# Attention and MLP in one kernel: the first unit's keys split ahead of their square sums, the first pair's left rows loaded alone, two weight loads and the LayerNorm scaling moved on GpSimd's queue, and the last tile stored in three groups

## The chip, the cores and the metric

The kernel runs on one core of a Trainium2 chip. The metric is the device time of one execution in microseconds. A profile is one execution taken by the hardware profiler; its times count from the first instruction (the span). In what follows PE is the matrix engine, DVE the vector engine, ACT the scalar engine, POOL is GpSimd, and SP the engine that mostly issues DMAs. PSUM is the memory that PE writes.

## The reference

```
q_n, k_n = rmsnorm(q, g_q), rmsnorm(k, g_k)        # over head_dim = 64
attn = softmax(q_n @ k_n.T / sqrt(64))
x = (attn @ v), heads side by side                 # batch 8, seq 448, 12 heads -> 768 columns
xn = (x - mean) / sqrt(var + 1e-6) * g_ln
out = x + relu(xn @ w_ch1) @ w_ch2                 # 768 -> 3072 -> 768
```

All inputs and the output are float32. The kernel works in float16 with float32 sums: keys are split into a high and a low half, so that the product with the queries loses little.

## The kernel before, in words

**Work.** Heads are handled in pairs, 6 pairs for each of 8 batches, 48 in all (p = 0 to 47). The tokens of a head are 384 "main" rows (three tiles of 128) and 64 "left" rows. The left rows of the two heads of a pair share one tile of 128. The inputs of one or two pairs form a unit u, which is loaded and prepared together: units 0 and 1 have one pair, all others two.

**Preparing a unit** is a set of one-letter steps (`pieces`, line 185): `b` begins; `a` and `c` square the keys and the queries on ACT (line 210); `d` and `e` sum the squares on DVE (L213); `gk`, `gq` or `g` take the inverse roots on ACT (L216, L218); `i` multiplies the keys by g_q times g_k, on DVE for units 0 to 2 and on POOL after that (L223; in unit 0 it first makes that product, L222); `j` rounds the keys to their high half, on POOL for units 1 to 4 and on ACT otherwise (L229, L231); `k` subtracts it to make the low half on DVE (L234); `l` scales the queries on DVE (L67); `m` duplicates them on DVE or POOL (L273); `z` casts the values on POOL (L279, L285).

**Attention of a pair.** `K` and `Q` transpose keys and queries on PE (L307 to L324) and copy them out of PSUM (L312 on DVE, L327 on ACT or L329 on DVE). `S p.i` multiplies one tile of keys by the queries (L346, or L349 and L350 for the left rows) and takes the exponential on ACT (L352, out to the tile E). Two PSUM buffers hold the scores, so a score waits until ACT has read the one two before. `V p.i` multiplies E by the values (L375, L377), and after the seventh the result is divided by its sums on DVE (L390 to L397).

**MLP of a batch.** `T` takes statistics (L528), `A` and `N` make the normalized rows on DVE (L543, L548, which read `gln`), `X` transposes them, and `R` takes the root. The first three blocks of the first product are written out as `U` (L642), the others are L599 with the ReLU at L601. The second product is L612: for each token tile and each half of 384 columns, 24 matmuls; then DVE adds the residual (L616) and the tile is stored (`store`). In the last batch the last tile (the left rows of two batches) comes last, in two halves of 384 columns, each stored by two DMAs on SP's queue (L657).

**What sets the order.** The first attention, up to the MLP of batch 0, is written out by hand in the list `ORDER`: it is walked once, and each engine executes its own share in that order. From then on the attention of batch b + 1 is woven into the MLP of batch b in steps. `load_first` (line 137) issues the loads of batch 0: ACT's queue takes the first pair's keys, SP's queue all else. Here the keys' and queries' left rows of all six pairs come in one call, which is two DMAs (one for each head of a pair, L135). In `ORDER`, `G` loads `gln`, `G2` scales it on POOL (L424), `L4` to `L7` load units 4 to 7 on SP, and `W0`, `W1`, `W2` load the thirds of w_ch1 from POOL's queue (L502); the halves of w_ch2 follow later (L507). At the end `flag` counts values that are out of bounds; its result decides whether a slow general version runs (it doesn't with these inputs). Two of its operations (L707, L709) are placed by the scheduler in DVE's stream right behind the first `i0`.

Each DMA from SP's or ACT's queue signals on one of eight semaphores, taken in turn. A DMA that takes a semaphore again waits on its queue until the earlier DMA on it has landed. In the kernel before, the first eight (the first pair's loads, all left rows, and g_q and g_k) wait for nothing.

Of the kernel before, what the change touches and what calls it, by code (L numbers as in the profile page):

```python
# [8 lines left out]
FP32 = mybir.dt.float32  # L9
FP16 = mybir.dt.float16  # L10
INT32 = mybir.dt.int32
ALU = mybir.AluOpType
AFT = mybir.ActivationFunctionType
AX = mybir.AxisListType
ENG = mybir.EngineType
PSUM = bass.MemoryType.PSUM
ts = bass.ts

B, H, S, D = 8, 12, 448, 64
DM, FF = 768, 3072  # L20
NDC, NFF = DM // 128, FF // 128
NPAIR = H // 2
# [11 lines left out]


ORDER = """
b0 c0 e0 a0 d0 b1 i0 gq0 a1 G L4 L5 j0 z0 k0 gk0 l0 i1 m0 d1 c1 K0 Q0 e1 b2 j1 g1 a2 S0.0 S0.1
S0.2 l1 m1 k1 c2 S0.3 d2 K1 e2 S0.4 V0.0 i2 S0.5 Q1 g2 j2 l2 V0.1 S0.6 S1.0 S1.1 S1.2 m2 b3
V0.2 a3 z2 V0.3 k2 c3 S1.3 S1.4 K2 V0.4 V0.5 Q2 V0.6 V1.0 S1.5 i3 W0 d3 S1.6 V1.1 e3 V1.2 S2.0
T0 V1.3 S2.1 K3 S2.2 Q3 S2.3 V1.4 S2.4 z3 V1.5 V1.6 S2.5 S2.6 V2.0 S3.0 g3 S3.1 V2.1 S3.2 j3  # L40
W1 k3 W2 G2 V2.2 l3 b4 S3.3 m3 S3.4 Q4 V2.3 V2.4 a4 K4 S3.5 V2.5 V2.6 S3.6 Q5 V3.0 S4.0 S4.1
K5 d4 c4 V3.1 V3.2 i4 V3.3 S4.2 V3.4 V3.5 S4.3 V3.6 V4.0 S4.4 S4.5 V4.1 S4.6 e4 j4 T1 V4.2 k4
g4 S5.0 S5.1 V4.3 V4.4 V4.5 l4 S5.2 S5.3 S5.4 K6 V4.6 S5.5 V5.0 V5.1 m4 z4 L6 b5 V5.2 S5.6 a5
i5 V5.3 V5.4 V5.5 Q6 V5.6 T3 S6.0 S6.1 S6.2 S6.3 T5 S6.4 V6.0 A V6.1 N0 V6.2 N1 V6.3 S6.5 V6.4
S6.6 X0 X1 U0 V6.5 c5 N2 X2 d5 U1 U2 R e5 V6.6 g5 j5 k5 l5 m5 z5 L7
""".split()
DMA_UNIT = 8
PE_SET = (DMA_UNIT + 1) % 2
# [4 lines left out]
K_MAX = 6.0e4  # L53
# [22 lines left out]
class _Fast:  # L76
# [60 lines left out]
    def load_first(self):  # L137
        nc = self.nc
        flat = self.hT.rearrange("p f n -> p (f n)").bitcast(FP32)
        t = [flat[:, 2688 * n:2688 * n + 2688].rearrange("p (w g d) -> p w g d", w=NPAIR, d=D)  # L140
             for n in range(2)]
        flat = self.sh.w2.rearrange("p f n -> p (f n)").bitcast(FP32)
        t.append(flat[:, 128:128 + 2688].rearrange("p (w g d) -> p w g d", w=NPAIR, d=D))
        main = lambda eng, n, p: self.load_main(eng, n, t[n][:, p, 0:6], 0, 2 * p, 2)
        left = lambda eng, n: self.load_left(eng, n, t[n][:, :, 6], 0, 0, H)
        for n, eng in ((0, nc.sync), (1, nc.scalar)):
            main(eng, n, 0)
            left(eng, n)
        for n in range(2):
            nc.sync.dma_start(self.sh.gg[:, n], self.gs[n].unsqueeze(0).broadcast_to([128, D]))  # L150
        for n, p in ((1, 1), (0, 1), (1, 2), (1, 3), (0, 2), (0, 3), (2, 0), (2, 1)):
            main(nc.sync, n, p)
        left(nc.sync, 2)
        for n, p in ((1, 4), (1, 5), (0, 4), (0, 5)):
            main(nc.sync, n, p)
        for p in range(2, NPAIR):
            main(nc.sync, 2, p)
        self.v_first = t[2]
        for u, (b, hs, m) in enumerate(UNITS):
            if b == 0:  # L160
                self.loads[u] = [x[:, hs // 2:hs // 2 + m].rearrange("p w g d -> p (w g) d")
                                 for x in t]
# [22 lines left out]
    def pieces(self, u):  # L185

        nc, sh = self.nc, self.sh
        m = UNITS[u][2]
        mh, g = 2 * m, 7 * m
# [16 lines left out]
        def square(n):  # L206

            o = c["khl" if n == 1 else "qn"].rearrange("p g e d -> p (g e d)").bitcast(FP32)
            c["sq", n] = o.rearrange("p (g d) -> p g d", d=D)
            nc.scalar.activation(c["sq", n], c["t"][n], AFT.Square)  # L210

# [7 lines left out]

        def kg():  # L220
            if u == 0:
                nc.vector.tensor_tensor(out=sh.gprod, in0=sh.gg[:, 0], in1=sh.gg[:, 1], op=ALU.mult)  # L222
            (nc.vector if u in DVE_KG else nc.gpsimd).tensor_tensor(  # L223
                out=c["t"][1], in0=c["t"][1],
                in1=sh.gprod.unsqueeze(1).broadcast_to([128, g, D]), op=ALU.mult)
# [63 lines left out]
        def vall():  # L289
# [7 lines left out]
                    e=lambda: total(0), gq=lambda: root(0), gk=lambda: root(1), g=root, i=kg,  # L297
# [109 lines left out]
    def first_attention(self):  # L407
        nc, gln = self.nc, self.sh.gln
        self.batch(0)
        self.load_first()  # L410
        nc.scalar.add_instruction(mybir.InstLoadActFuncSet(
            name=nc.get_next_instruction_name(), act_func_set_id=LN_EXP_SET))
        nc.scalar.activation(self.sh.warm, self.sh.ones, AFT.Ln)
        ln = {}
        for x in ORDER:
            key, n = x[0], x[1:]
            if x == "S6.0":
                self.batch(1)
            if key == "L":
                self.load_unit(int(n))  # L420
            elif x == "G":
                nc.sync.dma_start(gln, self.g_ln.unsqueeze(0).broadcast_to([128, DM]))
            elif x == "G2":
                nc.gpsimd.tensor_scalar(out=gln, in0=gln, scalar1=XS, scalar2=None, op0=ALU.mult)  # L424
            elif key == "W":
                c = int(n)
                self.load_w1(1024 * c, 1024 * c + 1024) if c < 3 else self.load_w2(c - 3)
            elif key in "SV":
                (self.scores if key == "S" else self.values)(*map(int, n.split(".")))
            elif key in "KQT":  # L430
                dict(K=self.trans_k, Q=self.trans_q, T=self.stats)[key](int(n))
            elif key in "ANXR":
                ln = ln or self.ln_ops(0)
                ln[x]()
            elif key == "U":
                self.up_first(int(n))
            elif key == "H":
                ps = self.ps_m.tile([128, 512], FP32, tag="mlp", name="psW")
                for _ in range(int(n)):
                    nc.tensor.matmul(ps[:, 0:384], self.sh.id16,  # L440
                                     self.v16.rearrange("p s h j d -> p (s h j d)")[:, 0:384],
                                     start=True, stop=True)
            else:
                self.prep_ops(int(x[-1]))[x[:-1]]()
# [143 lines left out]
    def mlp_chunks(self, b):  # L588

        nc, sh = self.nc, self.sh  # L590
        tiles = self.tok_tiles(b)
        n = len(tiles)
        N = 128 * n
        xnT, hT = self.xnT, self.hT

        def up(f):
# [4 lines left out]
            nc.scalar.activation(out=hT[:, f, 0:N], in_=ps[:, 0:N], func=AFT.Relu)  # L601

        cur = {}
        order = [(t, g) for g in range(2) for t in range(n)] if b == 0 else [
            (t, g) for t in range(n) for g in range(2)]

        def down(t, g, s):
            if s == 0:
                cur["ps"] = self.ps_m.tile([128, 512], FP32, tag="mlp", name="psC")
            ps = cur["ps"]  # L610
            for f in range(6 * s, 6 * s + 6):
                nc.tensor.matmul(ps[:, 0:384], hT[:, f, ts(t, 128)], sh.w2[:, f, ts(g, 384)],  # L612
                                 start=(f == 0), stop=(f == NFF - 1))
            if s == 3:
                x = tiles[t]
                nc.vector.scalar_tensor_tensor(  # L616
                    out=x[:, ts(g, 384)], in0=ps[:, 0:384], scalar=self.rs[:, b, t:t + 1],
                    in1=x[:, ts(g, 384)], op0=ALU.mult, op1=ALU.add)
                if t == n - 1:
                    self.store(b, t, g)  # L620
                elif g == 1:
                    self.late.append((b, t, 2))
            elif s == 1:
                for a in self.late:
                    self.store(*a)
                self.late = []
# [2 lines left out]
            yield 6 * N / 2.4, (lambda f=f: up(f))  # L629
        for t, g in order:  # L630
            for s in range(4):
                yield 6 * 160, (lambda t=t, g=g, s=s: down(t, g, s))

    def up_first(self, t):

# [9 lines left out]
            if t == 2:  # L645
                nc.scalar.activation(out=self.hT[:, f, 0:384], in_=ps[:, 0:384], func=AFT.Relu)

    def store(self, b, t, g):

        nc, out = self.nc, self.out  # L650
        cols = slice(0, DM) if g == 2 else slice(384 * g, 384 * g + 384)
        x = (self.xs[b][:, t] if t < 3 else self.xls[b // 2])[:, cols]
        if t < 3:
            nc.sync.dma_start(out[b, 0:384].rearrange("(p j) d -> p j d", j=3)[:, t, cols], x)
        else:
            for e in range(2):
                nc.sync.dma_start(out[b - 1 + e, 384:448, cols], x[64 * e:64 * e + 64])  # L657


    def upto(self, target):  # L660
# [40 lines left out]
    def flag(self):  # L701
# [2 lines left out]
        nc, sh = self.nc, self.sh  # L704
        n = B * NPAIR * 8
        rec = self.rec.rearrange("p n t e -> p (n t e)")
        nc.vector.tensor_reduce(out=sh.gmax, in_=sh.gprod, axis=AX.X, op=ALU.max,  # L707
                                apply_absolute_value=True)
        nc.vector.tensor_scalar(out=sh.gmax, in0=sh.gmax, scalar1=1.0 / K_MAX, scalar2=None,  # L709
                                op0=ALU.mult)  # L710
        good = self.p_m.tile([128, n], FP32, tag="xn", name="good", bufs=4)
        cnt = self.fix.tile([128, 3], FP32, name="cnt", tag="cnt")
        nc.vector.tensor_scalar(out=good, in0=rec, scalar1=REC_LO, scalar2=None, op0=ALU.is_ge)
# [202 lines left out]
```

## Time and profile before

| | us |
|---|---|
| median of 7 runs (lowest, highest) | 619.29 (618.34, 620.86) |
| time of the profiled execution | 623.42 |
| its span | 621.4 |
| PE busy in the span | 584.2 (94%) |
| ACT busy, DVE busy, POOL busy | 362.0, 290.2, 184.4 |
| mean granted PE clock | 0.988 |

A timeline line gives the start, the busy time, the engine, the source line, the operation, output<-inputs, shapes, how many instructions are merged, and in brackets how long the engine sat idle before and what ended that. SPq, POOLq and ACTq lines are DMAs being issued. In a line of windows the first numbers are the window and its length, then each engine's busy time, then the granted PE clock. A line of the waits names who waited for whom, the total, the number of times and the longest.

### The profile page before, as it was taken

The numbers are of one execution on the slowest core, as the hardware profiler recorded it, in microseconds if no ns is written. First come the engines' busy times: TensorE is split into PE (matmuls) and PEld (weight loads), VectorE is DVE, ScalarE is ACT, GpSimd is POOL, SyncE is SP. The second block draws the span as 40 slices with busy tenths as digits, with TensorE's granted clock in tenths as the row PEclk, the third lists the DMA queues.
The fourth block names the chain that finished last, engine by engine and source line by source line (L and its number), as shares of the span: only waits on it lengthen the run. The fifth ranks groups of instructions, "written<-read, shape, count | busy, mean of one in ns | idle before, by whom it ended". The sixth has DMA issues, their size and how long they took to land.

```text
span 621.4 us, 11453 instructions
## 1 busy us (share of the span) xinstructions
PE 584.2 (94%) x4476; PEld 345.9 (56%) x4476; DVE 290.2 (47%) x614; ACT 362.0 (58%) x697; POOL 184.4 (30%) x239
## 2 busy tenths in 40 slices
PE   1777999989999999999999999999999999999995
PEld 0455666645556666655556666655556666654563
DVE  4778867632454544652454544652454422450011
ACT  3978887517875189717775289627765277214200
POOL 0653432204535066605435066605422000000000
PEclk9979999989999999999999999999999999999998
DMA  7999499754387366757379495748434340030011
GB/s 187 265 193 224 109 221 220 157 144 129 87 81 180 110 149 147 150 130 143 77 79 174 115 149 149 147 129 147 101 53 109 90 61 2 26 102 0 2 52 55
DMA packets 131437, 75.29 MB, mean 121 GB/s; under 512 B 97456, under 2 KB 121680, under 8 KB 131376
## 3 DMA queue, kind: packets, MB, share of 16 engines
q1 hardware_dynamic: 114384, 45.38, 36.3%
q0 software_dynamic: 15920, 28.71, 20.9%
q8 instruction: 37, 0.61, 0.4%
q10 hardware_dynamic: 1072, 0.39, 0.2%
q14 instruction: 24, 0.20, 0.1%
HBM read 52.36 MB, written 11.01 MB: 102 GB/s over the span
## 4 chain that ended last, share of the span: by engine, by line
PE 87%; DVE 5%; ACT 3%; issue 1%; DMA 0%; ACTq 0%; DVEq 0%
PE psC L612 34%; PE psH L599 34%; PE psS L346 8%; PE oA L375 5%; PE oB L377 2%; PE psS L349 1%; PE psS L350 1%; ACT E L352 1%; DVE khl L234 1%; PE tr L310 1%; DVE ssq L213 1%; ACT qn L210 1%; DVE x L392 1%; DVE qn L67 1%; ACT khl L210 0%
## 5 line engine op out<-in xcount | busy, mean ns | idle before, releaser
L599 PE MATMUL psH<-xnT,w 128*128 128x512 f16 (+1 forms) x1134 | 243.5, 354 | 2.2 <-DMA xnT<-xn 2.2
L352 ACT ACTIVATE E<-psS,rr_all 128x448 f16<-128x448 f32 x336 | 207.2, 635 | 52.2 <-PE psS L346 45.5
L612 PE MATMUL psC<-w,hT 128*128 128x384 f16 x1344 | 234.6, 326 | 0.0
L601 ACT ACTIVATE hT<-psH 128x512 f16<-128x512 f32 (+1 forms) x189 | 104.0, 551 | 129.6 <-PE psH L599 126.9
L612 PEld LDWEIGHTS <-hT 128*128 128x128 f16 x1344 | 126.1, 98 | 75.7
L599 PEld LDWEIGHTS <-w 128*128 128x128 f16 x1134 | 102.9, 98 | 84.1 <-issue 4.8
L346 PE MATMUL psS<-qU,kU 128*128 128x448 f16 x288 | 101.6, 360 | 9.2 <-ACT E L352 7.5
L375 PEld LDWEIGHTS <-E 128*128 128x128 f16 x1008 | 71.2, 99 | 49.7 <-issue 3.9
L223 POOL TENSOR_TENSOR qkv<-qkv,gprod 128x896 f32<-128x896 f32 x21 | 43.8, 2087 | 98.4 <-ACT khl L210 54.6
L375 PE MATMUL oA<-v,E 128*128 128x65 f16 x864 | 67.3, 195 | 0.9 <-DVE x L392 0.8
L616 DVE SCALAR_TENSOR_TENSOR x<-psC,rs_all,x 128x384 f32<-128x384 f32 x48 | 29.0, 616 | 70.8 <-PE psC L612 70.3
L390 DVE RECIPROCAL rec_all<-oA 128x6 f32<-128x6 f32 x48 | 9.3, 195 | 98.4 <-PE oA L375 98.2
L377 PE MATMUL oB<-v,E 128*128 128x65 f16 x288 | 52.0, 194 | 0.1
L127 POOL DMA_DIRECT2D qkv<-in_k_dram x14 | 11.2, 801 | 134.5 <-ACT E L352 72.0
L213 DVE TENSOR_REDUCE ssq<-khl 128x14 f32<-128x896 f32 (+1 forms) x25 | 26.2, 1046 | 44.1 <-ACT khl L210 44.0
L346 PEld LDWEIGHTS <-kU 128*128 128x128 f16 x288 | 28.4, 99 | 26.5 <-issue 8.1
L213 DVE TENSOR_REDUCE ssq<-qn 128x14 f32<-128x896 f32 (+1 forms) x25 | 26.2, 1047 | 27.3 <-ACT qn L210 27.1
L67 DVE SCALAR_TENSOR_TENSOR qn<-qkv,rq 128x256 f16<-128x256 f32 (+1 forms) x72 | 26.8, 429 | 22.0 <-ACT rq L218 22.0
L377 PEld LDWEIGHTS <-E 128*128 128x128 f16 x336 | 32.7, 97 | 0.5 <-DVE xl L397 0.2
L392 DVE TENSOR_TENSOR x<-oA,rec_all 128x384 f32<-128x384 f32 x48 | 26.8, 558 | 1.5
L234 DVE TENSOR_TENSOR khl<-qkv,khl 128x896 f16<-128x896 f32 x21 | 22.8, 1084 | 8.0 <-ACT khl L231 5.7
L528 DVE BATCH_NORM_STATS2 stat<-x 128x6 f32<-128x256 f32 x72 | 26.1, 416 | 0.7
(99 smaller groups left out, 447.9 us busy)
## 6 DMA issues: line engine op xcount, KB each, us to landing
out_dram<-x SPq DMA_DIRECT2D x20, 384.0 KB, 2.5
qkv<-in_k_dram POOLq DMA_DIRECT2D x14, 384.0 KB, 3.9
qkv<-in_q_dram POOLq DMA_DIRECT2D x14, 384.0 KB, 5.1
qkv<-in_v_dram POOLq DMA_DIRECT2D x14, 384.0 KB, 6.4
w<-in_moe_w_ch_dram POOLq DMA_DIRECT2D x3, 1536.0 KB, 17.2
w<-in_moe_w_ch_dram POOLq DMA_DIRECT2D x2, 2304.0 KB, 29.2
qkv<-in_k_dram SPq DMA_DIRECT2D x7, 384.0 KB, 6.0
qkv<-in_q_dram SPq DMA_DIRECT2D x7, 384.0 KB, 5.5
```

The lines of the kernel that those rows point to most:

```text
L67: nc.vector.scalar_tensor_tensor(out=out, in0=x, scalar=8.0, in1=r.unsqueeze(2).broadcast_to([x.shape[0], g, D]), op0=ALU.mult, op1=ALU.mult)
L213: nc.vector.tensor_reduce(out=c["ssq"][:, n], in_=c["sq", n], axis=AX.X, op=ALU.add)
L223: (nc.vector if u in DVE_KG else nc.gpsimd).tensor_tensor(out=c["t"][1], in0=c["t"][1], in1=sh.gprod.unsqueeze(1).broadcast_to([128, g, D] ...
L234: nc.vector.tensor_tensor(out=c["khl"][:, :, 1], in0=c["t"][1], in1=c["khl"][:, :, 0], op=ALU.subtract)
L346: nc.tensor.matmul(ps[:, 0:S], c["main"][:, ts(i, 128)], q[:, ts(h, S)], start=True, stop=True)
L352: nc.scalar.activation(out=c["E"][:, i], in_=ps[:, 0:S], func=AFT.Exp, scale=self.rr[:, g:g + 1], bias=EXP_BIAS)
L375: nc.tensor.matmul(oA[:, t, cs], E[:, i, ts(t, 128)], rhs, start=(i == 0 and t == 0), stop=(i == 6 and t == 2))
L377: nc.tensor.matmul(oB[:, cs], E[:, i, 320:448], rhs, start=(i == 0), stop=(i == 6))
L392: nc.vector.tensor_tensor(out=x[:, :, 128 * hp:128 * hp + 128].rearrange("p t (e d) -> p t e d", e=2), in0=oA[:, :, :, 0:D], in1=rec[:, 0: ...
L599: nc.tensor.matmul(ps[:, 0:N], sh.w1[:, dc, ts(f, 128)], xnT[:, dc, 0:N], start=(dc == 0), stop=(dc == NDC - 1))
L601: nc.scalar.activation(out=hT[:, f, 0:N], in_=ps[:, 0:N], func=AFT.Relu)
L612: nc.tensor.matmul(ps[:, 0:384], hT[:, f, ts(t, 128)], sh.w2[:, f, ts(g, 384)], start=(f == 0), stop=(f == NFF - 1))
```

## The change

The diff, cut to its core. `ORDER` first:

```diff
-b0 c0 e0 a0 d0 b1 i0 gq0 a1 G L4 L5 j0 z0 k0 gk0 l0 i1 m0 d1 c1 K0 Q0 e1 b2 j1 g1 a2 S0.0 S0.1
-S0.2 l1 m1 k1 c2 S0.3 d2 K1 e2 S0.4 V0.0 i2 S0.5 Q1 g2 j2 l2 V0.1 S0.6 S1.0 S1.1 S1.2 m2 b3
-V0.2 a3 z2 V0.3 k2 c3 S1.3 S1.4 K2 V0.4 V0.5 Q2 V0.6 V1.0 S1.5 i3 W0 d3 S1.6 V1.1 e3 V1.2 S2.0
-T0 V1.3 S2.1 K3 S2.2 Q3 S2.3 V1.4 S2.4 z3 V1.5 V1.6 S2.5 S2.6 V2.0 S3.0 g3 S3.1 V2.1 S3.2 j3
-W1 k3 W2 G2 V2.2 l3 b4 S3.3 m3 S3.4 Q4 V2.3 V2.4 a4 K4 S3.5 V2.5 V2.6 S3.6 Q5 V3.0 S4.0 S4.1
-K5 d4 c4 V3.1 V3.2 i4 V3.3 S4.2 V3.4 V3.5 S4.3 V3.6 V4.0 S4.4 S4.5 V4.1 S4.6 e4 j4 T1 V4.2 k4
-g4 S5.0 S5.1 V4.3 V4.4 V4.5 l4 S5.2 S5.3 S5.4 K6 V4.6 S5.5 V5.0 V5.1 m4 z4 L6 b5 V5.2 S5.6 a5
+b0 a0 c0 G L4 L5 i0 j0 e0 k0 gq0 l0 b1 m0 a1 c1 K0 Q0 d0 gk0 S0.0 S0.1 i1 e1 d1 g1 z0 j1 l1 m1
+k1 b2 a2 S0.2 c2 S0.3 d2 K1 e2 S0.4 V0.0 i2 S0.5 Q1 g2 j2 l2 V0.1 S0.6 S1.0 S1.1 S1.2 m2 b3
+V0.2 a3 z2 V0.3 k2 c3 S1.3 S1.4 K2 V0.4 V0.5 Q2 V0.6 V1.0 S1.5 i3 W0 d3 j3 S1.6 V1.1 e3 V1.2
+S2.0 T0 V1.3 S2.1 K3 S2.2 Q3 S2.3 V1.4 S2.4 z3 V1.5 V1.6 S2.5 g3 S2.6 V2.0 S3.0 S3.1 V2.1 S3.2
+k3 V2.2 l3 b4 S3.3 m3 S3.4 V2.3 V2.4 a4 K4 Q4 S3.5 V2.5 V2.6 S3.6 Q5 V3.0 S4.0 S4.1 K5 d4 c4
+V3.1 V3.2 i4 W1 V3.3 S4.2 V3.4 V3.5 S4.3 V3.6 V4.0 S4.4 S4.5 V4.1 S4.6 e4 j4 W2 T1 V4.2 k4 g4
+S5.0 S5.1 V4.3 V4.4 V4.5 l4 S5.2 S5.3 S5.4 K6 V4.6 S5.5 V5.0 V5.1 m4 z4 G2 L6 b5 V5.2 S5.6 a5
 i5 V5.3 V5.4 V5.5 Q6 V5.6 T3 S6.0 S6.1 S6.2 S6.3 T5 S6.4 V6.0 A V6.1 N0 V6.2 N1 V6.3 S6.5 V6.4
-S6.6 X0 X1 U0 V6.5 c5 N2 X2 d5 U1 U2 R e5 V6.6 g5 j5 k5 l5 m5 z5 L7
+S6.6 X0 X1 U0 V6.5 c5 N2 X2 d5 U1 U2 R e5 V6.6 g5 j5 k5 l5 m5 z5 L7 M
```

`M` is the two operations at L707 and L709, taken out of `flag`. The loads:

```diff
-        left = lambda eng, n: self.load_left(eng, n, t[n][:, :, 6], 0, 0, H)
+        left = lambda eng, n, p=0, m=NPAIR: self.load_left(eng, n, t[n][:, p:p + m, 6], 0, 2 * p, 2 * m)
         for n, eng in ((0, nc.sync), (1, nc.scalar)):
             main(eng, n, 0)
-            left(eng, n)
+            left(eng, n, 0, 1)
+        left(nc.scalar, 1, 1, NPAIR - 1)
         for n in range(2):
             nc.sync.dma_start(self.sh.gg[:, n], self.gs[n].unsqueeze(0).broadcast_to([128, D]))
-        for n, p in ((1, 1), (0, 1), (1, 2), (1, 3), (0, 2), (0, 3), (2, 0), (2, 1)):
+        main(nc.sync, 1, 1)
+        left(nc.sync, 0, 1, NPAIR - 1)
+        for n, p in ((0, 1), (1, 2), (1, 3), (0, 2), (0, 3), (2, 0), (2, 1)):
             main(nc.sync, n, p)
```

The keys' squares of unit 0 go to a place of their own, because the high half of the keys is now written before their sum is taken:

```diff
             o = c["khl" if n == 1 else "qn"].rearrange("p g e d -> p (g e d)").bitcast(FP32)
+            if u == 0 and n == 1:
+                o = self.hT.rearrange("p f n -> p (f n)").bitcast(FP32)[:, 5376:5376 + g * D]
```

The last tile of the last batch (second halves split in two, one of each two stores on ACT's queue):

```diff
+            (t, g) for t in range(n) for g in (
+                ((0, 384), (384, 192), (576, 192)) if (b, t) == (B - 1, n - 1)
+                else ((0, 384), (384, 384)))]
...
-                    self.store(b, t, g)
+                    self.store(b, t, cols, nc.scalar if b == B - 1 else nc.sync)
...
-                nc.sync.dma_start(out[b - 1 + e, 384:448, cols], x[64 * e:64 * e + 64])
+                (eng if e else nc.sync).dma_start(out[b - 1 + e, 384:448, cols],
+                                                  x[64 * e:64 * e + 64])
```

Read engine by engine, DVE's stream differs in the first unit (the sums d0, e0 and d1 and the product i1 stand later), in `M`, in the order of the copies of Q4 and K4 and in one more L616 at the end. PE's stream differs in that K4 now stands ahead of Q4 and behind V2.3 and V2.4, and in the last tile. On POOL, j3 stands ahead of z3, W1 behind i4, W2 behind j4, and G2 behind z4. On ACT, a0 and c0 change places, the keys' root of unit 0 stands behind the copy of Q0, the root of unit 3 two exponentials earlier, and ACT issues two loads more at the start and three stores at the end; the first-pair loads on SP are shorter, with two more behind k's second pair. By the turn of the semaphores, g_k's load now waits for the landing of the first pair's main key rows, and ACT's last load for that of the main query rows.

More of the change, by code (lines that the diff above doesn't have):

```diff
@@ L221, in kg @@
             if u == 0:
-                nc.vector.tensor_tensor(out=sh.gprod, in0=sh.gg[:, 0], in1=sh.gg[:, 1], op=ALU.mult)
+                nc.vector.tensor_tensor(out=sh.gprod, in0=sh.gg[:, 0], in1=sh.gg[:, 1],
+                                        op=ALU.mult)
             (nc.vector if u in DVE_KG else nc.gpsimd).tensor_tensor(
@@ L434, in first_attention @@
                 ln[x]()
+            elif key == "M":
+                gmax = self.sh.gmax
+                nc.vector.tensor_reduce(out=gmax, in_=self.sh.gprod, axis=AX.X, op=ALU.max,
+                                        apply_absolute_value=True)
+                nc.vector.tensor_scalar(out=gmax, in0=gmax, scalar1=1.0 / K_MAX, scalar2=None,
+                                        op0=ALU.mult)
             elif key == "U":
@@ L603, in mlp_chunks @@
         cur = {}
-        order = [(t, g) for g in range(2) for t in range(n)] if b == 0 else [
-            (t, g) for t in range(n) for g in range(2)]
+        order = [(t, g) for g in ((0, 384), (384, 384)) for t in range(n)] if b == 0 else [
+            (t, g) for t in range(n) for g in (
+                ((0, 384), (384, 192), (576, 192)) if (b, t) == (B - 1, n - 1)
+                else ((0, 384), (384, 384)))]
         def down(t, g, s):
+            cols = slice(g[0], g[0] + g[1])
             if s == 0:
@@ L611, in down @@
             for f in range(6 * s, 6 * s + 6):
-                nc.tensor.matmul(ps[:, 0:384], hT[:, f, ts(t, 128)], sh.w2[:, f, ts(g, 384)],
+                nc.tensor.matmul(ps[:, 0:g[1]], hT[:, f, ts(t, 128)], sh.w2[:, f, cols],
                                  start=(f == 0), stop=(f == NFF - 1))
@@ L616, in down @@
                 nc.vector.scalar_tensor_tensor(
-                    out=x[:, ts(g, 384)], in0=ps[:, 0:384], scalar=self.rs[:, b, t:t + 1],
-                    in1=x[:, ts(g, 384)], op0=ALU.mult, op1=ALU.add)
+                    out=x[:, cols], in0=ps[:, 0:g[1]], scalar=self.rs[:, b, t:t + 1],
+                    in1=x[:, cols], op0=ALU.mult, op1=ALU.add)
                 if t == n - 1:
-                    self.store(b, t, g)
-                elif g == 1:
-                    self.late.append((b, t, 2))
+                    self.store(b, t, cols, nc.scalar if b == B - 1 else nc.sync)
+                elif cols.stop == DM:
+                    self.late.append((b, t, slice(0, DM)))
             elif s == 1:
@@ L631, in mlp_chunks @@
             for s in range(4):
-                yield 6 * 160, (lambda t=t, g=g, s=s: down(t, g, s))
+                yield 6 * g[1] / 2.4, (lambda t=t, g=g, s=s: down(t, g, s))
     def up_first(self, t):
@@ L646, in up_first, with store @@
                 nc.scalar.activation(out=self.hT[:, f, 0:384], in_=ps[:, 0:384], func=AFT.Relu)
-    def store(self, b, t, g):
+    def store(self, b, t, cols, eng=None):
         nc, out = self.nc, self.out
-        cols = slice(0, DM) if g == 2 else slice(384 * g, 384 * g + 384)
         x = (self.xs[b][:, t] if t < 3 else self.xls[b // 2])[:, cols]
@@ L706, in flag @@
         rec = self.rec.rearrange("p n t e -> p (n t e)")
[L707 to L710, printed above, removed]
         good = self.p_m.tile([128, n], FP32, tag="xn", name="good", bufs=4)
```

## The prediction

> **What bounds the kernel now.** I read the slices first.
>
> ```profile
> PE   1777999989999999999999999999999999999995
> ...
> ACT  3978887517875189717775289627765277214200
> ...
> PEclk9979999989999999999999999999999999999998
> ```
>
> From the fourth slice (62 us) PE is busy without a break, and nothing of the change touches its work there but the last tile. So the change is worth what it moves in the first 62 us and in the tail. Of the waits on PE between 62 and 611 us only one is over 1 us (2.2, at 131.9), and all issues there hang on earlier work; what the first 62 us gain is therefore passed on, if the weights still come in time.
>
> The windows of the first stage show where those 62 us are loose:
>
> ```profile
> 33.00:36.50 3.50, 1.85 (x13) 0.66 (x11) 3.43 (x4) 3.47 (x9) 3.48 (x4) 1.00 0.97 151
> 36.50:40.50 4.00, 2.52 (x28) 2.30 (x28) 2.38 (x4) 0.97 (x2) 3.35 (x2) 0.53 1.06 195
> 40.50:44.00 3.50, 3.50 (x35) 2.61 (x33) 2.14 (x6) 2.02 (x4) 0.00 (x0) 0.56 1.13 211
> 44.00:50.00 6.00, 4.24 (x59) 2.62 (x56) 5.78 (x11) 5.75 (x13) 0.93 (x1) 1.00 1.12 212
> ```
>
> Columns are PE, its weight loads, DVE, ACT, POOL, the clock. Before 36.5 and after 44 DVE and ACT are full. Between them ACT works 2.99 of 7.5 us and the clock is at half. The timelines of the engines tell why:
>
> ```profile
> 33.92 1.75 DVE L234 TENSOR_TENSOR khl<-hT,khl 128x896 f16<-128x896 f32 x1
> 35.60 1.70 DVE L67 SCALAR_TENSOR_TENSOR qn<-hT,rq 128x896 f16<-128x896 f32 x1
> 37.34 0.59 DVE L273 COPY qn<-qn 128x896 f16<-128x896 f16 x1
> ...
> 33.70 1.65 POOL L502 DMA_DIRECT2D w<-in_moe_w_ch_dram  x2
> 35.38 2.29 POOL L424 TENSOR_SCALAR gln<-gln 128x768 f32<-128x768 f32 x1
> ...
> 37.98 0.29 PE L321 MATMUL psQ<-id,qn 128*128 128x128 f16 x1 [2.02 <-DVE qn L273]
> ...
> 40.51 0.63 ACT L352 ACTIVATE E<-psS,rr_all 128x448 f16<-128x448 f32 x1 [3.04 <-PE psS L346]
> ```
>
> The three DVE steps of unit 3 (k3, l3, m3) take 1.75, 1.70 and 0.59; the same shapes stand elsewhere, with POOL idle, at 1.08, 1.08 and 0.39. Beside them POOL issues W1 and W2 and scales `gln`. PE waits 2.02 us for m3, because Q4 stands ahead of V2.3, V2.4 and K4, then runs at half clock (448 columns at 0.58 instead of 0.35), and ACT waits 3.04.
>
> **The middle (W1, W2, G2, Q4, j3, g3).** DVE is continuous from 29.37 to 33.89 (chain of waits), so k3 still starts at 33.92 in this profile's clock. Starts are 1.01 apart at full speed (62.16, 63.16 for the sums of this size; 66.18, 67.19 for k and l): k3 33.92, l3 34.93, m3 35.94 to 36.34, against 37.93 now: 1.6 earlier. PE does V2.3 and V2.4 (0.22) behind S3.4 (35.61), K4 at 36.4, Q4 at 36.95 (0.55 each at the full clock, as at 29.74 and 30.32), S3.5 at 37.5 instead of 39.89. ACT ends a4 at 37.47 in both, so the first exponential comes at 37.75 instead of 40.51. From there both bounds go on: DVE has the two copies (0.66, 0.62), the division after V2 (1.32), the copies of Q5 and K5, d4 (1.09), the division after V3, e4, and reaches the end of e4 at about 45.0 instead of 48.19, with ACT's five exponentials behind c4 done at 44.9. I take **-3.2**. Ends: -1.6 if only m3's own gain comes through (half clock as now), -4.8 if DVE also loses all its idle time between 37.93 and 48.19 (10.26 less 7.1 busy, plus 1.6).
>
> The half clock is part of this. It was granted from 36.75, after 3.4 us in which PE worked 1.64; the next-emptiest stretches of that length before 60 us, 2.2 to 2.4 busy, kept the full clock. With V2.3, V2.4 and K4 in the gap the stretch 33.3 to 36.75 has about 2.2, so I expect the full clock; where the 3.4 us fall is chance, and I give the half clock 20%. The Trainium skill ("TensorE: Matmul & The Clock Gate", "Why this matters for your kernels") says that gaps up to about 3 us between bursts do no harm; here a gap of 2.02 us among thin work went with a drop, so the row and the page differ. By the page the clock would have nothing to do with the gap and the middle would be worth its lower end.
>
> **What the moved work costs where it goes.** j3 (0.94) now runs at 31.4, after d3's end at 30.46, and z3 behind it to 33.85: free before k3. W1 and W2 are one issue each (0.83 to 1.02). W1 goes behind i4 (37.5 to 39.7), W2 behind j4, which waits for d4. Queued behind them are j4 and m4; DVE at those times does PSUM copies, divisions and sums, which the trace shows at equal length with POOL busy or idle (L392 0.56 always, L213 1.07 to 1.09). W0, issued at 30.32, lands at 43.45, W1 at 50.93, W2 at 58.62, one after the other at a full DMA share; W2 issued at 44 is still ahead of its turn. The eighth and sixteenth block of L599 need them after 70 and 80 us. Cost 0; if the cover were gone, the first would be late by what W1 lands after 67.
>
> G2 (2.29) behind z4 delays i5 and z5. Measured from l4's end at 51.16, m4, z4 and G2 take 0.94 + 1.5 + 2.29 and end at 55.9, 1.4 ahead of N0 (57.30), which reads `gln`. But i5 (2.08) now runs 55.9 to 58.0 and z5 (1.49) until 59.5, beside N0, N1 and N2 (0.95 each). DVE operations with two inputs in SBUF beside a POOL cast took 1.09 (L234, 72.61) or 1.46 (L67, 73.88) instead of 1.08; beside i's product no row shows one. N1 leads to X1 and U0, N2 has 1 us to spare. I take **+0.3**, nearest to the row at 73.88; ends 0 and +1.3 (all three at 1.6 times). The Trainium skill ("SBUF — State Buffer", "two separate sides") calls the shared port an exclusive lock that is held for a whole instruction. Here l3, started 0.22 after G2, ended 0.37 before it, so it was slowed, not shut out. By the page N1 would wait out casts already begun, and the term would be near +1.3.
>
> `M` (0.21 + 0.15) leaves the first unit, where L709 ended at 11.71 while k0 waited for ACT until 12.05, and goes behind m5 at 69.1; DVE has 0.52 idle in the next 4 us (before 71.66 and 72.61). Cost 0, at most +0.36 if d6 and e6 pass it on.
>
> **The start.** Four lines carry it:
>
> ```profile
> 10.51 0.23 DVE L222 TENSOR_TENSOR gprod<-w 128x64 f32<-128x64 f32 x1 [2.17 <-DMA w<-in_g_k_dram]
> ...
> 15.87 0.83 POOL L279 CAST v<-w 128x768 f16<-128x768 f32 x1 [14.55 <-DMA w<-in_v_dram]
> ...
> 17.75 0.56 POOL L229 CAST khl<-hT 128x448 f16<-128x448 f32 x1
> ...
> 18.34 0.95 DVE L234 TENSOR_TENSOR khl<-hT,khl 128x448 f16<-128x448 f32 x1 [1.17 <-POOL khl L229]
> ```
>
> Everything waits for g_k (issued 3.61, landed 6.8 later). Its issue now waits for the key rows, 0.75 + 3.9 = 4.65; on the other hand 256 packets of left rows, not 1536, are ahead of it (the DMA share falls only at 5.5), and the two g loads then took 2.4 to 2.8 from first to last. I estimate g_q landing at 7.2 and g_k at 9.5, 0.9 earlier; ends 1.1 later (the issue's delay) and 1.1 earlier. ACT's table load moves behind the second load's wait (4.3 + 0.64), 1.28 + 0.2, so its first square still starts near 6.5. From gprod to the first score now 5.45 us; without i1 (0.62) between l0 and m0 it is 4.9.
>
> But unit 1 takes the gain back: its k1 waits for j1, which POOL does behind z0, and z0 waits for the values. Their loads are issued behind one more wait for g_k (q2's turn) and two more left loads of 0.6 each, so they land about when they do now: I estimate 0.3 earlier. K1 (19.34) and all after it gain **-0.3**; ends -1.1 and +2.4 (the issue 1.1 later and 1.3 of two more places in the queue).
>
> **The tail.** Two lines of the timeline and one of the waits:
>
> ```profile
> 611.45 5.01 SPq L657 DMA_DIRECT2D out_dram<-xl  x4
> 614.70 0.62 DVE L616 SCALAR_TENSOR_TENSOR xl<-psC,rs_all,xl 128x384 f32<-128x384 f32 x1 [3.28 <-PE psC L612]
> ```
>
> ```profile
> SPq L884 <- SPq L884: 2.6, 1, 2.6
> ```
>
> After the last add SP issues two stores (615.35 to 616.46), branches, waits 2.6 and leads the end. Now the add has 192 columns: L67 took 0.42 for 256 and 0.285 for 128, 1.05 ns a column, so 0.2 less. SP issues one store, 0.59 less. 48 matmuls of 192 columns in place of 24 of 384 cost PE nothing if the pitch halves; transposes of 128 columns with a weight load each come every 0.057, so 0.08 is free; I allow +0.06. But ACT now reads the flag and branches behind its own store: 615.7 + 0.54, then up to 3.46 as PE's branch took: 619.7, about when SP is done. I take **-0.6**; ends -0.9 and 0.
>
> **Sum.** -0.3 - 3.2 + 0.3 - 0.6 = -3.8. The profiled execution took 623.42 (span 621.4 and 2.0 around it), 4.1 over the median 619.29; it would take 619.6, and the median **615.5**.
>
> **Rivals.**
> 1. *The clock still drops*, at another place in the thin stretch. Then the middle is worth 1.6 and the sum is -2.2: **617.1**. For it: PE stays thin from 33.5 to 36.4. Against: K4 comes 1.6 before Q4 did.
> 2. *The start pays as well and a second drop goes.* The half clock at 135.7 (3.4 us, so 1.7 lost) follows PE's wait of 2.2 at 131.9, and may miss it by chance: -1.1 - 3.2 - 0.6 - 1.7 = -6.6, **612.7**.
> 3. *The load queue holds up the values: slower.* The waits for g_q and g_k stand in front of k3 and q2, and so of all that is behind them on SP. If the values' left rows, now 16.65, land later by L, K1 is later by L, unit 2's loads too. Against the 3.5 gained elsewhere it decides from L = 3.5, landing at 20.2; it is slower by over 0.2% from 21.4. At 22.5, say: +5.8 - 3.5 = +2.3, **621.6**. Against: my bound is 2.4.
> 4. *The first 62 us don't pass it on*: ACT's chain at 67 to 74 or the load of w_ch2 (landed 96.42, needed at 99.3) takes it back; only the tail remains: **618.7**.
>
> **Chances.** Forecast 60%, from 614 to 617 by itself; rival 1 16%, rival 2 8%, rival 3 8%, rival 4 8%. 0.2% is 1.2 us, about what the runs can tell from no change. Rivals 3 and 4 split: slower 8%, same 9% (618.05 to 620.5), faster 83%. The range leaves out rival 3 and the far ends of 2 and 4: 612.9 to 618.8.
>
> **What would show it.** Right: L234 and L67 of unit 3 at 1.08, K4 ahead of Q4 with no wait over 0.5, the clock at 1.0 from 36 to 44, the end of e4 about 3.5 us earlier, K1 near 19.0, one store on SP behind the last add. Wrong: a clock of half there, values landing after 17.5, N0 to N2 at 1.5 each, PE waiting for w in L599 or L612.

## The result and the profile after

The changed kernel takes 616.85 us (median of 19 runs, 614.73 to 618.87), the kernel before 619.21 in the same comparison. The ratio is 0.9961, 95% interval 0.995 to 0.9971, or 2.4 us less (1.8 to 3.1). The forecast was 615.5, with 614 to 617 as its own range.

The profiled execution of the changed kernel took 619.82, with a span of 618.1 (before: 623.42 and 621.4). The slices of the page show the same picture as before from the fourth slice on, where PE is full:

```profile
PE   1687999999999999999999999999999999999995
...
ACT  3896887527765399627765399527765377214200
...
PEclk9898999999999999999999999999999999999998
```

Four windows of the first stage follow (columns PE, its weight loads, DVE, ACT, POOL, the clock, then the DMA share and GB/s). The first two are at the times of the two half-clock windows of before:

```profile
36.50:40.50 4.00, 3.72 (x53) 2.70 (x51) 3.48 (x8) 3.94 (x8) 1.34 (x1) 1.00 1.13 214
40.50:44.00 3.50, 2.74 (x45) 1.95 (x43) 3.34 (x8) 3.50 (x7) 2.49 (x4) 1.00 0.52 70
...
53.40:57.70 4.30, 2.26 (x37) 1.37 (x35) 4.30 (x9) 2.79 (x5) 4.24 (x4) 1.00 1.11 223
57.70:61.10 3.40, 3.40 (x38) 3.40 (x36) 0.88 (x2) 1.65 (x2) 0.71 (x1) 0.50 1.11 276
```

The hole at 36 to 44 is gone: ACT works 7.44 of 7.5 us where it worked 2.99, at the full clock. But there is a new half clock at 57.7, after a stretch in which PE works half of the time. Two groups of timeline lines, DVE's and PE's, show the middle as it is now:

```profile
35.26 1.09 DVE L240 TENSOR_TENSOR khl<-hT,khl 128x896 f16<-128x896 f32 x1
36.27 1.08 DVE L67 SCALAR_TENSOR_TENSOR qn<-hT,rq 128x896 f16<-128x896 f32 x1
37.39 0.39 DVE L279 COPY qn<-qn 128x896 f16<-128x896 f16 x1
...
37.59 0.22 PE L313 MATMUL tr<-id,khl 128*128 128x128 f16 x1
...
37.98 0.22 PE L327 MATMUL psQ<-id,qn 128*128 128x128 f16 x1
```

k3, l3 and m3 take 1.09, 1.08 and 0.39, and PE goes from K4 to Q4 without a wait. Yet k3 starts at 35.26, 1.34 later than before. The lines of the first unit and of POOL tell where the first 0.7 of it comes from; the other 0.6 is a half clock between K1 and k3:

```profile
9.47 0.23 DVE L227 TENSOR_TENSOR gprod<-w 128x64 f32<-128x64 f32 x1 [6.60 <-DMA w<-in_g_k_dram]
...
16.57 0.83 POOL L285 CAST v<-w 128x768 f16<-128x768 f32 x1 [15.25 <-DMA w<-in_v_dram]
...
18.45 0.56 POOL L235 CAST khl<-hT 128x448 f16<-128x448 f32 x1
...
20.05 0.29 PE L313 MATMUL tr<-id,khl 128*128 128x128 f16 x1 [3.15 <-DVE khl L240]
```

The g weights come 1.04 earlier, but the values 0.70 later (their first load is issued at 10.64 instead of 8.79), and everything behind them (z0, j1, k1, K1) moves with the values: K1 starts at 20.05 instead of 19.34. Adding up the pair of profiled executions by what starts when:

| stretch | before | after | difference |
|---|---|---|---|
| up to K1 | 19.34 | 20.05 | +0.7 |
| K1 to k3 | 14.58 | 15.21 | +0.6 (half clock at 26.98 to 30.4) |
| k3 to the end of e4 | 14.27 | 10.01 | -4.3 |
| end of e4 to N0 | 9.11 | 9.12 | 0 |
| N0 to the end of N2 | 2.81 | 3.86 | +1.05 |
| end of N2 to the first L599 (now L611) | 3.55 | 4.76 | +1.2 (half clock at 57.7 to 61.1) |
| from there to the sixth of DVE's adds (L616, now L631), 132 | 68.75 | 68.56 | -0.2 |
| to the seventh, 180 | 50.37 | 47.88 | -2.5 (no half clock at 136: 1.7; PE's wait there 0.8 shorter) |
| to the end | 438.65 | 438.60 | -0.05 |

From the seventh add to the first half of the last tile every add keeps its distance in all profiles of this study to 0.02 us; all differences lie ahead of 180 us and in the tail.

The -2.5 in the last row but one is not the change's. From the first L599 to the seventh add the kernel before takes 119.12 us and the changed one 116.44; but r5 below, which has the old order everywhere up to there, takes 116.66, and e1, with the changed one, 117.36. PE's wait at 131 us is for a DMA transpose and scatters alike with the old order and the new: 2.21 before, 1.45 in r5, 1.41 in the changed kernel, 2.15 in e1. Of the 3.4 us between the two profiled spans some 0.9 are left for the change, the 1.8 that its two half clocks take included.

### The profile page after: what moved, and what is told of

It reads as the page before. It is cut to its first block, busy times and chain, and to the rows that moved or that the text cites. A ratio compares the mean times of both kernels' runs of the same rounds, so it can differ in the third digit from the quotient of the medians.

```text
span 618.1 us, 11521 instructions
## 1 busy us (share of the span) xinstructions
PE 582.2 (94%) x4500; PEld 347.9 (56%) x4500; DVE 290.0 (47%) x615; ACT 361.8 (59%) x697; POOL 186.2 (30%) x239
## 4 chain that ended last, share of the span: by engine, by line
PE 86%; ACT 5%; DVE 4%; DMA 1%; issue 1%; SPq 0%; ACTq 0%; DVEq 0%
PE psC L627 34%; PE psH L611 34%; PE psS L352 7%; PE oA L381 5%; ACT E L358 2%; PE oB L383 2%; PE psS L355 1%; PE psS L356 1%; DMA qkv<-in_k_dram 1%; PE psU L657 1%; ACT qn L215 1%; PE tr L316 1%; DVE khl L240 0%; DVE xn L560 0%; DVE x L398 0%
## 5 line engine op out<-in xcount | busy, mean ns | idle before, releaser
L611 PE MATMUL psH<-xnT,w 128*128 128x512 f16 (+1 forms) x1134 | 242.1, 353 | 1.4 <-DVE x L631 1.4
L627 PE MATMUL psC<-w,hT 128*128 128x384 f16 (+1 forms) x1368 | 234.6, 323 | 0.0
L627 PEld LDWEIGHTS <-hT 128*128 128x128 f16 x1368 | 127.7, 98 | 74.2
L611 PEld LDWEIGHTS <-w 128*128 128x128 f16 x1134 | 102.5, 98 | 82.4 <-issue 2.4
L631 DVE SCALAR_TENSOR_TENSOR x<-psC,rs_all,x 128x384 f32<-128x384 f32 x48 | 29.0, 616 | 70.8 <-PE psC L627 70.3
L67 DVE SCALAR_TENSOR_TENSOR qn<-qkv,rq 128x256 f16<-128x256 f32 (+1 forms) x72 | 26.8, 429 | 19.6 <-ACT rq L223 19.5
```

What stands on the lines that cost most here:

```text
L67: nc.vector.scalar_tensor_tensor(out=out, in0=x, scalar=8.0, in1=r.unsqueeze(2).broadcast_to([x.shape[0], g, D]), op0=ALU.mult, op1=ALU.mult)
L611: nc.tensor.matmul(ps[:, 0:N], sh.w1[:, dc, ts(f, 128)], xnT[:, dc, 0:N], start=(dc == 0), stop=(dc == NDC - 1))
L627: nc.tensor.matmul(ps[:, 0:g[1]], hT[:, f, ts(t, 128)], sh.w2[:, f, cols], start=(f == 0), stop=(f == NFF - 1))
L631: nc.vector.scalar_tensor_tensor(out=x[:, cols], in0=ps[:, 0:g[1]], scalar=self.rs[:, b, t:t + 1], in1=x[:, cols], op0=ALU.mult, op1=ALU.add)
```

## The experiments

All were compared with the kernel before on the same chip. The two columns in the middle come from each one's profile; the last names the half clock from the first full clock (21.8 to 29.5 us into the span) to 600 us.

| kernel | median | ratio (95%) | k3 to end of e4 | N0 to N2 | half clock |
|---|---|---|---|---|---|
| before | 619.2 to 620.0 | 1 | 14.27 | 2.81 | 36.8 (6.8 us), 135.7 |
| changed | 616.85 | 0.9961 (0.995 to 0.9971) | 10.01 | 3.86 | 27.0, 57.7 |
| e1_tail_old | 618.60 | 0.9989 (0.9974 to 1.0003) | 9.73 | 3.85 | none |
| e2_start_old | 617.45 | 0.9967 (0.9953 to 0.9982) | 9.70 | 3.86 | none |
| e3_j1_first | 616.82 | 0.9952 (0.9932 to 0.9971) | 9.92 | 3.85 | 25.8, 56.5 |
| e4_g2_early | 616.58 | 0.9946 (0.9927 to 0.9964) | 9.70 | 2.81 | 53.4 |
| r5_tail_alone | 619.43 | 0.9985 (0.997 to 1.0) | 14.34 | 2.81 | 37.5 (6.8 us) |
| r6_q4_first | 618.37 | 0.9978 (0.9962 to 0.9994) | 10.37 | 3.84 | none |
| r7_gw_back | 617.39 | 0.9956 (0.9938 to 0.9974) | 10.51 | 2.80 | 26.5 |
| r8_j1_g2 | 615.54 | 0.9922 (0.9899 to 0.9944) | 9.70 | 2.80 | none |
| x1_k4_alone | 617.90 | 0.9969 (0.9954 to 0.9984) | 11.16 | 2.81 | none |
| x2_warm | 618.53 | 0.9973 (0.9959 to 0.9988) | 11.83 | 2.81 | none |
| x3_best_old_tail | 614.67 | 0.9917 (0.9892 to 0.9943) | 9.70 | 2.81 | none |
| x4_g1_early | 615.73 | 0.993 (0.9904 to 0.9955) | 10.14 | 2.80 | none |

**The middle, one half undone at a time.** r6 puts Q4 ahead again and leaves POOL's moves; r7 puts W1, W2 and G2 back and leaves K4 ahead (j3 and g3 stay where the change put them):

```diff
 # r6_q4_first
-m3 S3.4 V2.3 V2.4 a4 K4 Q4 S3.5
+m3 S3.4 Q4 V2.3 V2.4 a4 K4 S3.5
 # r7_gw_back
-k3 V2.2 l3 ... i4 W1 ... j4 W2 ... m4 z4 G2 L6
+W1 k3 W2 G2 V2.2 l3 ... i4 ... j4 ... m4 z4 L6
```

> The changed kernel with Q4 ahead of V2.3, V2.4 and K4 again, as before; POOL's moves stay. Theory: the middle's gain has two parts, the DVE steps of unit 3 beside an idle POOL (m3 1.3 us earlier after k3) and K4's transposes in the wait for m3 (0.8); this kernel loses the second: from k3's start to the end of e4 10.5 us instead of 9.7 to 10.0 (14.27 in the kernel before), 617.7, ratio 0.9975. Rival 1: the order is worth nothing once m3 is early: 616.9. Rival 2: the order is what kept the clock up; then the clock drops at 36 to 40 us again and it takes 619.

> The changed kernel with W1, W2 and G2 at their old place on POOL (around k3 and l3); K4 stays ahead of Q4. Theory: k3, l3 and m3 take 1.75, 1.70 and 0.59 again, m3 ends 1.5 later, the stretch from k3 to the end of e4 takes 11.2 to 11.5 us; N0 to N2 go back to 2.81 us, which gives 1.05 of it back, so the kernel takes 617.3, ratio 0.997. Rival: the slow DVE steps are nearly the whole of the middle (clock and ACT's wait follow from them): 13.5 us or more from k3 to the end of e4, 619.5, ratio 1.0.

PE's wait for m3 is this line in r6 and the next in r7:

```profile
38.02 0.23 PE L327 MATMUL psQ<-id,qn 128*128 128x128 f16 x1 [0.74 <-DVE qn L279]
```

```profile
38.50 0.23 PE L327 MATMUL psQ<-id,qn 128*128 128x128 f16 x1 [0.66 <-DVE qn L279]
```

Before it was 2.02. In both the clock stays up and the stretch is within 0.8 us of the changed kernel's. r6 is near its theory: POOL's moves without the order of PE bring 3.9 of the 4.3 us. r7 is better than its theory, in part by chance: l3 and m3 are slow again (1.71 and 0.58), but k3 takes 1.09, because the half clock at 26.5 put k3 off (15.3 us after K1, in x1 below 14.6) while POOL's issues came as early as in x1 (14.3 and 14.4 us after K1). Its ratio can't be told from the changed kernel's, and N0 to N2 give back 1.05 there: moving W1, W2 and G2 shows no gain on top of the new order of PE.

**The order alone, and the clock alone.** Both are the kernel before with one edit:

```diff
 # x1_k4_alone
-S3.3 m3 S3.4 Q4 V2.3 V2.4 a4 K4 S3.5
+S3.3 m3 S3.4 V2.3 V2.4 a4 K4 Q4 S3.5
 # x2_warm (H11: eleven matmuls that nobody reads)
-S3.3 m3 S3.4 Q4 V2.3
+S3.3 m3 S3.4 H11 Q4 V2.3
```

> The kernel before with one thing changed: V2.3, V2.4 and K4 stand ahead of Q4. W1, W2 and G2 stay beside k3 and l3. New theory, from the two runs that undid one half of the middle each: either half alone keeps PE's wait for m3 under 1 us and the clock up, and so gives most of the 4.3 us. Then from k3's start to the end of e4 it takes 10.5 us instead of 14.27, N0 to N2 stay at 2.81, and this one edit is worth what the whole change is worth: 616.5, ratio 0.995. Rival, the forecast's reading: without the DVE steps made faster m3 is still 1.6 late, and the gain is 2 at most: 617.5 or more, ratio 0.997.

> The kernel before with eleven matmuls of 384 columns added on PE between S3.4 and Q4, whose result nobody reads: they fill most of PE's wait for m3 and change no order and nothing on the other engines. If the half clock is what made the stretch long: it stays at full clock there, k3's start to the end of e4 takes 11 to 12 us instead of 14.27, ratio 0.996. If the wait itself made it long: 14 us, ratio 1.0.

In x1 DVE's steps are as slow as before and PE still waits:

```profile
34.49 1.74 DVE L234 TENSOR_TENSOR khl<-hT,khl 128x896 f16<-128x896 f32 x1
36.15 1.71 DVE L67 SCALAR_TENSOR_TENSOR qn<-hT,rq 128x896 f16<-128x896 f32 x1
...
38.53 0.23 PE L321 MATMUL psQ<-id,qn 128*128 128x128 f16 x1 [1.37 <-DVE qn L273]
```

Nevertheless the clock stays up, and the stretch takes 11.16 us, 3.1 less than before. The 3.1 are more than the 2 that the rival allowed. But the ratio, 0.9969, is the rival's number; its interval includes the whole change's 0.9961 and leaves out the theory's 0.995. So the order alone gets much of the change, and not shown is that it gets all. In x2 nothing is reordered; the timeline and the windows show idle time filled:

```profile
36.26 1.95 PE L440 MATMUL psW<-v,id 128*128 128x384 f16 x11
38.42 0.23 PE L321 MATMUL psQ<-id,qn 128*128 128x128 f16 x1 [0.21 <-DVE qn L273]
```

```profile
36.50:40.50 4.00, 3.79 (x47) 2.61 (x46) 3.26 (x6) 2.06 (x4) 3.80 (x2) 1.00 1.11 205
40.50:44.00 3.50, 2.97 (x52) 2.28 (x50) 3.35 (x7) 3.36 (x6) 0.00 (x0) 1.00 1.11 206
```

m3 is as late as before, Q4 starts no earlier after k3 than before (4.04 against 4.06), and yet the stretch takes 11.83 instead of 14.27: in this pair of profiles these 2.4 us are the half clock and nothing else. The mean granted clock over all runs of this comparison points the same way (0.9934 before, 0.9968 in x2), and so does the ratio: 1.7 us less (0.7 to 2.5). The rival, that the wait itself was the cost, falls.

**The start.** e2 takes back the loads and the first unit's order; e3 lets POOL do j1 ahead of z0:

```diff
 # e3_j1_first
-i1 e1 d1 g1 z0 j1 l1 m1
+i1 e1 d1 g1 j1 z0 l1 m1
```

> The changed kernel with its start as before: the loads of load_first and the order of the first unit, up to K1, of the kernel before; middle, LN scaling and tail as changed. Theory: the new start costs 0.7 us (K1 at 20.05 instead of 19.34, since the values' rows land behind two more left loads and j1 stands behind their cast), so this kernel is 0.7 faster than the changed one: 616.1, ratio 0.995, with K1 near 19.35. Rival: what the first pair gains (its first score at 14.53 instead of 15.96) is passed on in ACT's queue and the start is worth something: 617.2 or more.

> The changed kernel with j1 ahead of z0 in the order, so that on POOL the rounding of unit 1's keys no longer waits for the values. Theory: K1 waits for k1, k1 for j1, and j1 only for POOL; then k1 follows l1 on DVE at 17.9 and K1 starts at 18.9, 1.1 earlier than in the changed kernel, and what follows on DVE is 1.1 earlier as well: 615.8, ratio 0.9945. Rival: j1 was not the last thing missing; unit 2's loads (landed at 17.7 to 18.9) or ACT's squares set the pace, and the time stays at 616.9.

Landings scatter between executions by over 1 us, so the profiles are averaged here: with the old start (before, e2, r5, x1, x2) the g weights' product starts at 10.64, the cast of the values at 16.07, K1 at 19.53; with the new one (changed, e1, e4, r6, r7) at 9.95, 16.64 and 20.11; with j1 first as well (e3, r8, x3) K1 starts at 19.01. In e3 POOL's line that held K1 up comes two microseconds earlier:

```profile
16.42 0.56 POOL L235 CAST khl<-hT 128x448 f16<-128x448 f32 x1 [15.10 <-DMA hT<-in_k_dram]
16.92 0.83 POOL L285 CAST v<-w 128x768 f16<-128x768 f32 x1
```

So in the span the new start costs 0.6, and waiting behind z0 is what makes it cost. e3's median, 616.82, is nevertheless its rival's figure; its ratio, 0.9952, is nearer to the theory's 0.9945, with an interval that holds both. Outside the span the new start saves something: run time less span is 2.0 on average before and 2.2 in e2, against 1.8 in the changed kernel. That leaves +0.3, which e2's ratio can't tell from 0 (undoing the start: +0.0006, with about 0.0018 either way); e2's expected gain of 0.7 did not show.

One thing more differs behind the new start. From K1 to k3 all five profiles with the old start take 14.58 us, and the full clock begins at 22.7 to 23.8 and holds. With the new start six of nine take 15.2 to 15.3: in three the clock drops again at 25.8 to 27.0 (changed, e3, r7), in three it becomes full only at 28.0 to 29.5 (e4, r6, r8). That is 0.5 us on average, not in the sum above. Whether the new start causes it or these six were chance isn't settled; e2's ratio shows no such gain.

**The LN scaling.** e4 moves G2 to where POOL stands idle and DVE reads PSUM; r8 joins it with j1:

```diff
 # e4_g2_early
-V3.1 V3.2 i4 W1 ... m4 z4 G2 L6
+V3.1 V3.2 i4 G2 W1 ... m4 z4 L6
```

> The changed kernel with the LN scaling (G2) behind i4 on POOL, 8 us earlier, where DVE copies from PSUM and divides. Theory: the changed kernel's N0 to N2 took 3.86 us instead of 2.81 because z5 ran beside them, and z5 was there because of G2's 2.14 us; so N0 to N2 take 2.85 here and the first product starts 1.0 earlier: 615.9, ratio 0.9947. Rival: G2 costs the same wherever it stands; it then slows the sum of unit 4's squares and the copies at 41 to 43.5 us (more than 1.3 instead of 1.09 for the sum) or delays j4 and W1, and the time stays at 616.9.

> The changed kernel with both repairs: j1 ahead of z0 on POOL, and G2 behind i4. Theory: the two are independent, K1 starts 1.1 earlier after the first product of the g weights (8.6 us instead of 9.8 to 10.8) and N0 to N2 take 2.81, so the profile's adds come 2.1 earlier where the clock drops alike, and the kernel takes 614.9, ratio 0.993. Rival: the second gain is lost where PE waits for the transposes at 131 us, or in one more drop of the clock: 615.9, ratio 0.9947.

The timeline of the kernel before, of the changed kernel and of e4:

```profile
57.30 2.81 DVE L548 SCALAR_TENSOR_TENSOR xn<-x,stat,gln 128x768 f16<-128x768 f32 x3
...
56.01 0.82 POOL L279 CAST v<-qkv 128x768 f16<-128x768 f32 x1
```

```profile
54.39 3.86 DVE L560 SCALAR_TENSOR_TENSOR xn<-x,stat,gln 128x768 f16<-128x768 f32 x3
...
52.90 2.08 POOL L229 TENSOR_TENSOR qkv<-qkv,gprod 128x896 f32<-128x896 f32 x1
54.93 1.55 POOL L285 CAST v<-qkv 128x768 f16<-128x768 f32 x1
56.43 1.98 POOL L291 CAST vl<-qkv 64x128 f16<-64x128 f32 x2
```

```profile
54.28 2.80 DVE L560 SCALAR_TENSOR_TENSOR xn<-x,stat,gln 128x768 f16<-128x768 f32 x3
```

In e4 z5 is done when N0 starts, and N0 to N2 take what they took before; the sum of unit 4's squares keeps its 1.09. In the profile the theory held and its rival fell; the ratio, 0.9946, is the theory's, though its interval reaches the changed kernel's. r8 is faster than both kernels: 0.9922, near its theory's 0.993, its interval clear of the changed kernel's.

**The tail.** e1 is the changed kernel with the old last tile, r5 the kernel before with the new one, x3 is r8 with the old one:

```diff
 # e1_tail_old, x3_best_old_tail
-((0, 384), (384, 192), (576, 192)) if (b, t) == (B - 1, n - 1)
+((0, 384), (384, 384)) if (b, t) == (B - 1, n - 1)
...
-self.store(b, t, cols, nc.scalar if b == B - 1 else nc.sync)
+self.store(b, t, cols, nc.sync)
```

> The changed kernel with its last tile as before (two halves of 384 columns, all stores on SP's queue). The forecast's term for the tail was -0.6 us. Theory: the tail gave nothing, since in the changed profile the time from the start of the last add to the end of the span is 6.66 us against 6.68 before, so this kernel takes as long as the changed one (616.9, ratio 0.996). Rival: the tail is worth its 0.6 and the one profiled execution hides it; then 617.5, ratio 0.997, and 7.2 us from the last add's start to the end.

> The kernel before with nothing but the changed last tile (three groups, one of each two last stores on ACT's queue). Undoing the tail in the changed kernel left its profile's tail almost as it was (10.62 us from the add before the last one to the end, against 10.30 to 10.65 in the profiles with the new tail) but its median lay 1.7 us above the changed kernel's. Theory A, by the profiles: the tail is worth 0.2, this kernel takes 619.0 where before takes 619.2 (ratio 0.9997). Theory B, by the median: it is worth 1.5, ratio 0.9976, because the landing of the last stores, which the end waits for, is late in many executions that were not profiled for a page.

> The version with both repairs (j1 ahead of z0, G2 behind i4), with the last tile as in the kernel before. Third measurement of the tail: by the profiles so far it is worth 0.25 us (10.1 to 10.57 us from the add before the last one to the end, mean 10.4, against 10.6), by the medians of the first two 1 to 1.5. Then this kernel takes 615.8 (0.2 over the repaired one), or 616.8.

From the add before the old last one to the end, five profiles with the old tail take 10.62 to 10.77 (mean 10.69), nine with the new one 10.10 to 10.65 (mean 10.37): 0.3 less. By the ratios the tail is worth 1.7 (e1), 0.9 (r5) and -0.3 (x3), each with 0.9 to 2.1 either way; e1 lies above both figures expected of it, r5 between its two, x3 below both. The profiles say 0.3, the three ratios weighed by their intervals 1.1; these runs do not settle it.

**One step further.** x4 is r8 with g1 ahead of the first scores (`i1 e1 d1 g1 S0.0 S0.1 j1 z0`).

> The repaired version with the inverse roots of unit 1 (g1) ahead of the first two scores, so that on ACT they no longer stand behind two exponentials. Theory: l1 waited for them (17.3 in the run with j1 alone), k1 stands behind l1 on DVE and K1 behind k1; K1 then comes 8.0 us after the product of the g weights instead of 8.6 to 9.0, with the first exponentials 0.8 later, which PE's wait before K1 covers: 614.8, ratio 0.991. Rival: the exponentials put off fill ACT's queue behind K1, and nothing is gained: 615.5.

K1 came 8.4 us after the weights' product (x3 8.6, r8 9.0), not the 8.0 expected. From K1 to the end of e4 it took 24.9 where x3 took 24.3 and r8 25.0, and the ratio is no better than r8's (the intervals overlap). A gain isn't shown, which is what the rival said; its reason isn't shown either.

## Why the prediction was right or wrong

The direction was right, and so was the point it hung on: the hole at 36 to 44 us closes, and from 62 us on nothing takes it back. The sum was too large by 1.4 us. That it was no worse is in part luck: the middle gave 1.1 more than forecast, the start, the moved work and the tail together some 1.65 less. Step by step:

- **The middle, forecast -3.2 (ends -1.6 and -4.8): -4.3.** The steps showed as named (1.09, 1.08, 0.39; no wait at Q4; full clock; e4's end 2.9 earlier although k3 started 1.3 later). But the cause was split wrongly. The forecast gave 1.6 to the faster DVE steps as the part that is safe, and the clock a supporting role with 20% to lose. x2 gets 2.4 from the clock alone and x1 3.1 from the new order with the steps still slow; r6 gets 3.9 from POOL's moves with the old order. So the two halves of the edit don't add up: what they have in common is that in its profile either one keeps the clock up, and that is the bulk.
- **W1, W2, G2, forecast 0 and +0.3 (0 to +1.3): 0 and +1.05.** The weights came in time. N0, N1 and N2 took 1.40, 1.57 and 1.04. The value was taken from the nearest row (1.46 beside a cast), for one of three operations, where i5 and z5 lie beside all but the last; and the upper end, all three at 1.6 times, is 1.7 and not 1.3. The trace of before also had a dearer row: l2 (L67, 23.33) took 1.71 beside the cast of j2. The prediction's estimate by the Trainium skill's "SBUF — State Buffer" ("two separate sides") was 1.3, which is nearer, and its rule fits here: the operations took turns. i5 ends at 54.98 and N0 0.81 behind it, z5's first cast 0.69 behind N0, N1 0.81 behind that cast. The step that failed is the inference from one row, l3 beside G2, that such operations are slowed and not shut out; G2 is the odd one in these traces, the casts and the product do shut N0 and N1 out.
- **The start, forecast -0.3 (-1.1 to +2.4): +0.6 in the span, some -0.25 outside it.** The failing step is "they land about when they do now: I estimate 0.3 earlier": the g weights did come 0.7 earlier, but the values 0.6 later, behind two more loads of left rows. The chain g_k, values, z0, j1, k1, K1 was right.
- **The tail, forecast -0.6 (-0.9 to 0): between -0.3 and -1.1.** SP's branch comes 0.8 earlier after the last matmul (1.00 us instead of 1.85), as worked out. The wait behind it grew from 2.6 to 3.2 us in the profiled pair and takes part of that back:

```profile
SPq L895 <- SPq L895: 3.2, 1, 3.2
```

- **Rival 1 (the clock drops elsewhere, 617.1)** did happen in the profiled execution, at 27.0 and 57.7, though not in the place meant. The median, 616.85, is nearer to its 617.1 than to the forecast's 615.5, but not for its reason: the middle was worth 4.3 and not 1.6. The drop at 57.7, 1.2 us, is probably helped along by the change: it follows the stretch in which the slowed N0 to N2 keep PE waiting, and of the five profiles with such N0 to N2 (changed, e1, e2, e3, r6) two have it. **Rival 2's** drop at 135.7 is luck: of all 14 profiles only that of before has it, and r5, with the same order there, has not. **Rivals 3 and 4** did not come: the values landed 0.6 later, not 3.5, and the gain is passed on.

With the terms as measured: +0.3 (start) - 4.3 + 1.05 - 0.3 = -3.2, and -2.0 where the clock drops at 57.7. The median's -2.4 lies between; what the clock takes between K1 and k3 is in neither.

## What to carry to other kernels

Where PE is idle in a stretch that is thin anyway, ask first what else it could do there: a transpose that is ready, put ahead of one that waits, got 3.1 of the middle's 4.3 us in the profile (x1) without touching the slow producer. Two edits that keep the same clock up don't add: try each alone. Work moved off one busy place on POOL is paid for where it lands, so move it to where the other engine reads PSUM (e4), and not to the nearest gap. Of a load list, follow the last load that something waits for, not the first.

## What the runs showed of the hardware

- **The clock went with how much PE worked in a stretch, not with the longest gap.** Within an execution the records change only at multiples of 3.41 us from each other. In the 14 profiles, warm stretches of that length in which PE worked 1.2 to 1.64 us (five) were all followed by half clock; of 28 with 1.73 to 2.22 four were; with more, none. The stretch ahead of the drop at 57.7 had no gap over 1.0 us, and one in x1 with a gap of 1.69 us and 1.73 of work kept the clock. What decides between 1.73 and 2.22 isn't shown. The Trainium skill ("TensorE: Matmul & The Clock Gate", "Why this matters for your kernels") counts gaps of up to about 3 us as harmless; these runs do not agree.
- **Where the grid lies differs from execution to execution, for no reason that a line shows.** The first full clock came between 21.8 and 29.5 us (up to it the transposes of the keys stand 0.107 us apart, at the full clock 0.056), and single runs of the changed kernel differ by 4 us; so a drop in one profile is evidence only with others beside it.
- **Run time less span differs between kernels** (1.6 to 2.2 us), without a line in the profile that says why.
- **DVE operations with two inputs in SBUF and POOL's casts and products took turns, in whole operations.** Beside the chain i5, N0, z5, N1 above, l2 in the kernel before ends 0.94 us behind the end of the cast j2 (24.10), beside which it had started at 23.33. Only l3 beside G2 does not fit: it started 0.22 behind it and ended 0.37 ahead of it.
- **Beside POOL's DMA issues k3 took 1.74 in x1 and 1.09 in r7**, where the issues began 0.2 and 1.1 us ahead of it. What decides this was not tried.
